# Attention's P V product: from two column groups and two rounds a step to four column groups and three rounds per two steps

## The chip, the cores and the metric

The kernel runs on one core of a Trainium2 chip. The metric is the device time of one execution in microseconds (us), the median over several runs; lower is better. Where the text names engines, PE is TensorE (PEld its weight loads, which the profile lists by themselves), DVE is VectorE, ACT is ScalarE, POOL is GpSimd and SP is the engine that issues the DMAs.

## The reference

One transformer-like block over 2048 tokens of width 512: adaptive layer norm and 32-head attention with 16 channels a head, then a second modulated layer norm and a token-shift MLP. The part that the change touches:

```python
qkv = (x @ wqkv).reshape(B, S, 3, H, Dh).transpose(2, 0, 3, 1, 4)   # S=2048, H=32, Dh=16
q, k, v = qkv[0], qkv[1], qkv[2]
scores = einsum("bhqd,bhkd->bhqk", q, k) * (Dh ** -0.5)
p = softmax(scores, axis=-1)
o = einsum("bhqk,bhkd->bhqd", p, v)                # "P V" below
return o.transpose(0, 2, 1, 3).reshape(B, S, D) @ wo
```

The products are computed to nearly fp32 precision: an fp32 operand is split into a coarse part and a remainder, and products of the parts are added up.

## The kernel before

**Tiling.** Queries come in 4 chunks of 512 (`ci`); heads come in 16 pairs. A unit is one chunk with one head pair, so there are 64 units. Within a unit the 2048 keys are walked in 16 tiles of 128; one key tile of one unit is a step, numbered `s` from 0 to 1023. A step does the following for its two heads `j`:

- L883: two score matmuls `sc` (keys by queries, 128 x 512), which stand in different row groups of PE.
- L867: beside them two matmuls `mb` for the step 24 further on. Their only purpose is the row maximum of each query, which DVE takes at L863 and which is later put into the score operands as an additional row.
- L879: ACT takes the exponential of each score tile and writes it as a 32-bit integer into the tile `pt`. `pt` has five buffers, so step `s` takes the buffer of step `s - 5`.
- L931 (`p_low`): POOL rewrites the low 16 bits of every element of `pt` in place as an fp16 number. The upper 16 bits already read as a (tiny) fp16 number. So `pt` holds P in two fp16 halves, interleaved. When the schedule expects POOL to be over 0.8 us later than ACT, ACT does the work instead, in two pieces of 512 columns (it shows under the helper's line L114).
- L946 (`pv_part`): the P V matmuls. `v` stands in `vst`, in 128 columns for the upper and 128 for the lower half. A head's 64 columns are three bf16 parts of v (16 columns each), a column of ones (which gives the softmax denominator) and zeros. For the lower half the same columns are stored again, multiplied by 2^-39. Each matmul has 64 weight columns, 512 moving columns and writes 64 partitions of one PSUM bank, head 0 the upper and head 1 the lower 64. A pair of matmuls for the two heads is called a round here. A step has two rounds: `(s, 0)` with the upper halves of P and `(s, 1)` with the lower halves, which needs `p_low` to be done. 1024 steps give 2048 rounds, 4096 matmuls.

After a unit, ACT copies the bank out (L960), PE transposes it (`ot`, L971), and DVE and POOL add the three parts up and divide by the sum (L978, L988, L982).

**What sets the order.** One Python scheduler (`Sched`) writes the instructions of all engines in a fixed order; it keeps a modelled time for each engine. The attention loop walks blocks of three score pairs (`GRP`, one and a half steps). A block is emitted as: its rows (`sc` and `mb`), then the P V rounds (`col`) that belong to the block two before (`LAG`), then "fill" work on PE, for which each step has a fixed budget. Fill is everything else: in the first chunk the q, k and v projections and the preparation of the later weights, in chunks 1 to 3 the output projection and the MLP of the chunk before, and the `ot` transposes. PE, ACT, DVE and POOL execute their lists in order, so a late instruction holds up all that stands behind it on its engine. When the modelled bank or P half is not ready in time, `gap` puts in fill work earlier. After the last step, the MLP of the last chunk runs by itself.

**Where v comes from.** `v_weights` (L707) loads and splits the columns of `wqkv` for v, in two groups of 256; `v_tiles` (L667) multiplies, ACT, DVE and POOL make the three bf16 parts (L700 to L704) and the result goes to DRAM (`Vs`). It comes back as `vst`, 1 MB for a unit. The first v tiles must be back before the first P V round.

Of the kernel before, what the change touches and what calls it, by code (L numbers as in the profile page):

```python
# [33 lines left out]
VLO = 2.0 ** -39  # L34
# [13 lines left out]
CROW, CCOL, CIN, CMID, COUT = 232.0, 249.0, 105.0, 95.0, 67.0  # L48
# [6 lines left out]
GRP = 3  # L55
LACT = 800.0
# [231 lines left out]
def kernel(ctx, tc, A_x, A_wqkv, A_wo, B_w1, B_w2, B_w3, B_w4, c, w_mod, out):  # L288
# [44 lines left out]


# [5 lines left out]
    dve.memset(mhalf, -0.5)  # L340
    mone = con.tile([P, 4], F32, name="mone")
# [10 lines left out]
    Vs = dr.tile([NP, P, NKT, 256], BF16, name="Vs")  # L352
# [174 lines left out]
    npool = [0]  # L527
# [122 lines left out]

    vt = []
    for i in range(NV):
        t = qp.tile([P, H // 4, 2, 2, 64], BF16, name=f"vt{i}")
        for l in range(2):
            pool.memset(t[:, :, l, :, 48:64], 0.0)
            pool.memset(t[:, :, l, :, 48:49], VLO if l else 1.0)
        vt.append(t)
# [9 lines left out]
    def v_tiles(w, a, kts):  # L667
        wh, wl = halves(w, KT)
        for kt in kts:
# [11 lines left out]
            v = w[:, :, 0]  # L681
# [3 lines left out]
            def rest(v=v, b3=b3, r=r, b=b):  # L685
                dve.tensor_tensor(r, b3, v[:, :, :, 0:16], op=OP.subtract)
                sch.free(b)

            def store(kt=kt, w=w):
                vrs[0] -= 1  # L690

                def gone():
                    vlive.remove(kt)
                    if kt % 4 == 3:
                        done.add(("v", a, kt // 4))
                e = sch.dma(dma.dma_start, Vs[8 * a:8 * a + 8, :, kt, :].rearrange("a p n -> p a n"),
                            w.rearrange("p a l b n -> p a (l b n)"))
                sch.after(e, gone)

            sch.chain(("A", cA(256), lambda v=v, b3=b3: act.activation(v[:, :, :, 0:16], b3, AF.Copy)),  # L700
                      ("D", cD(256), rest),
                      ("A", cA(256), lambda v=v, r=r: act.activation(v[:, :, :, 16:32], r, AF.Copy)),
                      ("G", cG(256), lambda v=v, r=r: pool.tensor_tensor(v[:, :, :, 32:48], r, v[:, :, :, 16:32], op=OP.subtract)),
                      ("A", cA(768), lambda v=v, w=w: act.activation(w[:, :, 1, :, 0:48], v[:, :, :, 0:48], AF.Copy, scale=VLO)),  # L704
                      (None, 0, store), prio=VP, bank=b)

    def v_weights(a):  # L707
        return split_weights([A_wqkv[:, 2 * D + a * 256:2 * D + (a + 1) * 256]])
# [23 lines left out]
    def pieces_load():  # L732
        yield lambda: ("v", 0, 2) in done
        for i, (nm, src, nk, n) in enumerate(pieces):
            if i == order["wo"][0]:
                yield from mod_gen((2, garow, 0.0))
# [4 lines left out]
            for c in range(2):  # L741
                yield sch.wait(5000.0)
# [4 lines left out]
    def pieces_gen():  # L747
        while True:
# [7 lines left out]
            ops = []  # L756
            if nm in rows:
                ops.append(("G", cG(), lambda f=f, r=rows[nm]: pool.tensor_tensor(f, f, r, op=OP.mult)))
# [39 lines left out]
    for g in (mod_cols(), ln1_T(), qk_first(hi, lo), weights_gen(), qkv_gen(0, 1), qkv_gen(1, len(todo))):  # L798
        sch.add(g)
# [35 lines left out]
    def load_v(u):  # L835
        vst[u] = at.tile([P, NKT, 2, 128], BF16, name="vst", tag="vst", bufs=2)
        if u > 1:
            sch.dma(dma.dma_start, vst[u].rearrange("p k l n -> p k (l n)"), Vs[units[u][1]])

    def load_first_v(u, i):  # L840
        k = slice(4 * i, 4 * i + 4)
        sch.dma(dma.dma_start, vst[u][:, k].rearrange("p k l n -> p k (l n)"), Vs[units[u][1], :, k])
# [95 lines left out]
    def pv_part(s, i):  # L938
        u, kt = divmod(s, NKT)
        if kt == 0 and i == 0:  # L940
            pv[u] = ap_.tile([P, CH], F32, name="pv", tag="v", bufs=1)
        p, v = pt[s].bitcast(F16), vst[u]

        def mms():
            for j in range(2):
                te.matmul(pv[u][64 * j:64 * j + 64, :], v[:, kt, i, 64 * j:64 * j + 64], p[:, j, 1 - i::2],  # L946
                          start=(kt == 0 and i == 0), stop=(kt == NKT - 1 and i == 1), skip_group_check=True)
        e = sch.put("P", CCOL, 0.0, mms)
        if i:
            pt.pop(s)  # L950
            e_low.pop(s)
            if kt == NKT - 1:
# [11 lines left out]
    def o_fin(u, ac, ready):  # L964
# [9 lines left out]
        sm = at.tile([P, 8, DH], F32, name="sm", tag="sm", bufs=2)  # L974
        rc = at.tile([P, 8, 1], F32, name="rc", tag="rc", bufs=2)

        def sums():
            dve.reduce_sum(sm, bv[:, :, 0:48].rearrange("p th (a d) -> p th d a", a=3), axis=AX.X)  # L978
            sch.free(b)

        def fin():
            pool.tensor_tensor(osb[ci][:, :, pr * 32:pr * 32 + 32].rearrange("p t (h d) -> p t h d", d=DH),  # L982
                              sm.rearrange("p (t h) d -> p t h d", h=2),
# [489 lines left out]
```

## Time and profile before

| what | value |
|---|---|
| runs | 2198.15 us median of 3 (2196.1 to 2198.7) |
| profiled execution | 2190.31 us, of which the span is 2188.5 us |
| PE busy | 2070.5 us, 95% of the span |
| POOL busy | 1735.1 us, 79% |
| DVE busy | 1638.3 us, 75% |
| ACT busy | 1533.1 us, 70% |
| first P V matmul | at 107.8 us |
| last P V matmul | starts at 2023.1 us |

The page gives busy times by engine and by groups of equal instructions (line, engine, operation, output<-input, count, then busy us and mean ns of one, then idle time of the engine just before them and its releasers). A matmul's duration in the trace is its latency, about 0.39 us for 512 columns; successive matmuls overlap, so their cost is read from the distance between starts. A view of stages gives busy time of each engine in a window. The chain of waits is followed back from the last instruction, at each step to what released it. Times within the trace count from the start of the span.

### The profile page before, as it was taken

What the parts mean: (1) busy time and instruction counts of PE and PEld (TensorE: products, weight loads), DVE (VectorE), ACT (ScalarE), POOL (GpSimd) and SP (SyncE); (2) the same over time, 40 slices, a digit from 0 to 9 for tenths busy, and PEclk for the clock granted to TensorE, in tenths of its full rate; (3) what the DMA queues carried; (4) which work ended last, traced back from release to release, by engine and by line L of the source; (5) the groups of instructions that cost most, each with busy time, mean ns of one, the idle gap of its engine ahead of it and who ended that gap; (6) DMA issues with size and microseconds to landing.
All of it is one profiled execution on the core that took longest, in us unless ns stands there. A gap on an engine that the chain in (4) does not pass through costs nothing.

```text
span 2188.5 us, 37190 instructions
## 1 busy us (share of the span) xinstructions
PE 2070.5 (95%) x12400; PEld 1162.6 (53%) x12400; DVE 1638.3 (75%) x2916; ACT 1533.1 (70%) x3268; POOL 1735.1 (79%) x1680
## 2 busy tenths in 40 slices
PE   6889999998899999999999999999899999999899
PEld 4645554554445555554445545555455555554688
DVE  6757777778898877778997877777888777773654
ACT  6456886668868777767767778677677767868353
POOL 3358897689978988888879989788779988888341
PEclk9889999999999999999999999999999999999999
DMA  5788887577453443535434344344524543443332
GB/s 199 190 240 263 238 220 210 170 206 218 129 181 95 114 145 103 153 94 167 99 91 114 95 125 133 105 114 104 162 77 114 151 115 92 137 95 116 135 136 82
DMA packets 201711, 313.36 MB, mean 143 GB/s; under 512 B 85520, under 2 KB 137232, under 8 KB 177296
## 3 DMA queue, kind: packets, MB, share of 16 engines
q1 hardware_dynamic: 201520, 310.98, 50.0%
q8 instruction: 99, 1.62, 0.3%
q14 instruction: 92, 0.75, 0.1%
HBM read 243.27 MB, written 67.11 MB: 142 GB/s over the span
## 4 chain that ended last, share of the span: by engine, by line
PE 67%; DVE 10%; POOL 7%; ACT 6%; DMA 6%; issue 3%; SPq 1%; POOLq 0%; ACTq 0%; DVEq 0%
PE pv L946 18%; PE mb L867 12%; PE sc L883 10%; PE w L320 7%; PE w L318 6%; PE w L316 6%; POOL pt L931 4%; DVE mx L863 4%; ACT pt L879 3%; DMA vst<-Vs 1%; SPq L93 1%; PE ot L971 1%; DMA wst<-in_A_wqkv_dram 1%; DMA wr<-Ws 1%; DMA kst<-Ks 1%
## 5 line engine op out<-in xcount | busy, mean ns | idle before, releaser
L863 DVE TENSOR_REDUCE mx<-mb 128x1 f32<-128x512 f32 x2048 | 1282.6, 682 | 295.9 <-PE mb L867 273.2
L931 POOL TENSOR_SCALAR pt<-pt 128x1024 f16<-128x1024 uint16 x1007 | 1339.6, 1363 | 198.8 <-ACT pt L879 194.8
L879 ACT ACTIVATE pt<-sc 128x512 int32<-128x512 f32 x2048 | 1078.1, 601 | 385.0 <-PE mb L867 322.3
L867 PE MATMUL mb<-kst,qtl 48*128 48x512 f32 x2048 | 722.0, 448 | 41.1 <-DMA kst<-Ks 9.2
L883 PE MATMUL sc<-qtl,kst 64*128 64x512 f32 x2048 | 693.9, 439 | 5.6 <-DVE sm L978 2.3
L946 PE MATMUL pv<-pt,vst 128*64 128x512 f16 x4096 | 610.7, 399 | 32.0 <-POOL pt L931 25.2
L867 PEld LDWEIGHTS mb<-kst,qtl 48*128 48x128 f32 x2048 | 341.3, 195 | 202.6 <-DVE mx L863 43.2
L883 PEld LDWEIGHTS sc<-qtl,kst 64*128 64x128 f32 x2048 | 334.4, 187 | 140.5 <-issue 45.0
L946 PEld LDWEIGHTS <-vst 128*64 128x64 bf16 x4096 | 178.9, 108 | 341.8 <-issue 265.3
L316 PE MATMUL w<-A,wr 128*128 128x256 f32 (+2 forms) x576 | 174.7, 303 | 3.0 <-ACT A L310 3.0
L318 PE MATMUL w<-A,wr 128*128 128x256 f32 (+2 forms) x576 | 175.9, 305 | 1.5 <-DVE A L306 1.3
L320 PE MATMUL w<-A,wr 128*128 128x256 f32 (+2 forms) x576 | 172.7, 300 | 0.0
L1223 POOL TENSOR_TENSOR g<-xs,g 128x256 fp32r<-128x256 f32 (+2 forms) x144 | 103.7, 721 | 81.1 <-ACT g L1222 80.7
L318 PEld LDWEIGHTS w<-A,wr 128*128 128x128 f32 x576 | 111.6, 194 | 37.0 <-issue 34.1
L316 PEld LDWEIGHTS w<-A,wr 128*128 128x128 f32 x576 | 111.8, 194 | 29.3 <-issue 18.3
L320 PEld LDWEIGHTS w<-A,wr 128*128 128x128 f32 x576 | 111.6, 194 | 23.7 <-issue 23.7
L316 PE MATMUL w<-wr,g 128*128 128x512 f32 x288 | 121.9, 423 | 0.1
L320 PE MATMUL w<-wr,g 128*128 128x512 f32 x288 | 120.6, 419 | 0.3 <-POOL g L1223 0.3
L318 PE MATMUL w<-wr,g 128*128 128x512 f32 x288 | 118.1, 410 | 0.0
L1232 DVE SCALAR_TENSOR_TENSOR sq<-sq,w 128x256 f32<-128x256 f32 (+1 forms) x108 | 43.4, 403 | 71.3 <-ACT xs L1228 63.4
L1238 POOL TENSOR_TENSOR xs<-xs,sq 128x256 f32<-128x256 f32 (+1 forms) x108 | 75.9, 704 | 5.7 <-ACT sq L1237 5.2
L1143 POOL TENSOR_TENSOR trs<-tmv,mhalf 128x1 f32<-128x1 f32 x48 | 33.5, 701 | 54.1 <-DVE tmv L1140 54.1
(130 smaller groups left out, 2049.1 us busy)
## 6 DMA issues: line engine op xcount, KB each, us to landing
wr<-Ws SPq DMA_DIRECT2D x80, 1024.0 KB, 5.2
vst<-Vs SPq DMA_DIRECT2D x62, 1024.0 KB, 6.5
kst<-Ks SPq DMA_DIRECT2D x126, 384.0 KB, 6.7
Vs<-vt SPq DMA_DIRECT2D x32, 512.0 KB, 4.4
qtl<-Qs SPq DMA_DIRECT2D x128, 96.0 KB, 4.8
Ws<-wq SPq DMA_DIRECT2D x40, 256.0 KB, 5.6
Ws<-wst SPq DMA_DIRECT2D x40, 256.0 KB, 5.1
wst<-in_B_w_dram SPq DMA_DIRECT2D x36, 256.0 KB, 5.4
```

The source lines that it names most:

```text
L316: te.matmul(o, lh, rh, start=first, stop=False)
L318: te.matmul(o, lh, rl, start=False, stop=False)
L320: te.matmul(o, ll, rh, start=False, stop=last)
L863: end = sch.crit("D", 605, e + PX, lambda: dve.reduce_max(mxs[u][:, j, g, c:c + 1], b, axis=AX.X))
L867: return ready, lambda: te.matmul(b, lhs, kst[u % 3][r, c * CH:(c + 1) * CH], start=True, stop=True), after
L879: ea = sch.crit("A", 480, e + PX, lambda: act.activation(pt[s][:, j], b, AF.Exp))
L883: return ready, lambda: te.matmul(b, kst[u % 3][r, kt * P:(kt + 1) * P], qst[u][r], start=True, stop=True), after
L931: e_low[s] = XP["G"] + sch.crit("G", 1345, ready, lambda: pool.tensor_scalar(o, i, 0.5, 1.0, op0=OP.mult, op1=OP.mult))
L946: te.matmul(pv[u][64 * j:64 * j + 64, :], v[:, kt, i, 64 * j:64 * j + 64], p[:, j, 1 - i::2], start=(kt == 0 and i == 0), stop=(kt == NKT ...
L1223: ("G", cG(n), lambda: pool.tensor_tensor(lo, xs, hi, op=OP.subtract)), (None, 0, end))
L1232: dve.scalar_tensor_tensor(sq, sq, 1.0 / GELU_A, b, op0=OP.add, op1=OP.mult)
L1238: ("G", cG(n), lambda: pool.tensor_tensor(xs, xs, sq, op=OP.mult)), *tail_ops, bank=b)
```

## The change

**The P V matmuls.** The upper halves keep their arithmetic: 64 columns of v for each head. They are now issued as two matmuls of 32 columns for each head, so a round with the upper halves of one step is four matmuls in four column groups of 32 (two of the four stream the same P). The lower halves use a single fp16 copy of v in place of the three bf16 parts: 16 columns of v and one column of ones. So one head and one step need only one column group, and a round with lower halves takes two heads of two steps, `s` and `s + 1`, at once: four matmuls with 17 or 25 weight columns (the 25 have 8 zero columns in front, so that results add up onto the right partitions). The order is upper `s`, upper `s + 1`, lower of both. The count goes from 2048 rounds of two matmuls to 1536 rounds of four, that is from 4096 to 6144 matmuls, each with a weight load.

**A bound for fp16.** For v to fit fp16, the columns of the v weights are divided by a bound. `bounds` and the new part of `v_weights` form it from the modulation and the absolute weights: four DVE passes, eight fp32 matmuls with 256 columns (`vb`), some small DVE work and four POOL multiplications. The rows of `wo` are multiplied by the same bound later (four ACT passes), so that the output stays the same.

**Smaller parts.** `Vs` and `vst` have 192 columns in place of 256. Per v tile ACT makes the fp16 copy (256 columns) and no longer the copy by 2^-39 (768 columns). The sum over the three parts now takes the denominators along (136 in place of 128 outputs), and the reciprocal follows it. The constant that the schedule takes for a round goes from 249 to 240 ns, and the preparation of the later weights waits 3.5 us between loads in place of 5.

```diff
-CROW, CCOL, CIN, CMID, COUT = 232.0, 249.0, 105.0, 95.0, 67.0
+CROW, CCOL, CIN, CMID, COUT = 232.0, 240.0, 105.0, 95.0, 67.0
...
-    Vs = dr.tile([NP, P, NKT, 256], BF16, name="Vs")
+    Vs = dr.tile([NP, P, NKT, 192], BF16, name="Vs")
...
-            sch.chain(("A", cA(256), lambda v=v, b3=b3: act.activation(v[:, :, :, 0:16], b3, AF.Copy)),
+            sch.chain(("A", cA(256), lambda v=v, b3=b3: act.activation(v[:, :, :, 0:DH], b3, AF.Copy)),
+                      ("A", cA(256), lambda vl=vl, b3=b3: act.activation(vl[:, :, :, 8:8 + DH], b3, AF.Copy, scale=1.0 / VHI)),
                       ("D", cD(256), rest),
...
-                      ("A", cA(768), lambda v=v, w=w: act.activation(w[:, :, 1, :, 0:48], v[:, :, :, 0:48], AF.Copy, scale=VLO)),
...
+            sch.chain(("D", 1200, lambda x=f.bitcast(F32), t=t: dve.scalar_tensor_tensor(
+                t, x, -1.0, x, op0=OP.mult, op1=OP.max)), mark(keys[i]), ready=e)
+        yield lambda: keys[0] in done and keys[1] in done and "gb" in done and sch.room()
+        b = dbank("vb")[:, :256]
+        for k in range(KT):
+            te.matmul(b, gb[:, k], ab[k // 2][:, k % 2 * 256:k % 2 * 256 + 256], start=(k == 0), stop=(k == KT - 1))
...
+                sch.chain(("G", cG(), lambda f3=f3: pool.tensor_tensor(f3, f3, vb[:, None, :].to_broadcast([P, 2, 256]),
+                                                                       op=OP.mult)),
+                          *split_chain(f, w[:, 0, c], w[:, 1, c], mark(keys[2 + i])), ready=sch.T["D"] + XX)
...
-                yield sch.wait(5000.0)
+                yield sch.wait(3500.0)
...
-    def pv_ready(s, i):
+    def pv_ready(s, lo):
 
-        return e_low[s] if i else max(e_hi.pop(s), v_free[0] if s % NKT == 0 else 0.0)
+        return max(e_low[s], e_low[s + 1]) if lo else max(e_hi.pop(s), v_free[0] if s % NKT == 0 else 0.0)
...
             for j in range(2):
-                te.matmul(pv[u][64 * j:64 * j + 64, :], v[:, kt, i, 64 * j:64 * j + 64], p[:, j, 1 - i::2],
-                          start=(kt == 0 and i == 0), stop=(kt == NKT - 1 and i == 1), skip_group_check=True)
+                for i in range(2):
+                    r = 64 * j + 32 * i
+                    if lo:
+                        n = 9 + DH if i else 1 + DH
+                        c = 128 + 32 * j + 9 + DH
+                        te.matmul(acc[r:r + n, :], v[:, kt + i, c - n:c].bitcast(F16), pt[s + i].bitcast(F16)[:, j, 0::2],
+                                  start=False, stop=kt == NKT - 2, skip_group_check=True)
+                    else:
+                        te.matmul(acc[r:r + 32, :], v[:, kt, r:r + 32], pt[s].bitcast(F16)[:, j, 1::2],
+                                  start=kt == 0, stop=False, skip_group_check=True)
...
-        if i:
-            pt.pop(s)
-            e_low.pop(s)
+        if lo:
+            for i in range(2):
+                pt.pop(s + i)
+                e_low.pop(s + i)
...
+    pvs = [x for s in range(0, NS, 2) for x in ((s, 0), (s + 1, 0), (s, 1))]
...
-        col = [divmod(x, 2) for x in blocks[k - LAG] if x >= 0] if k >= LAG else []
+        if k >= LAG and (k % CPER == 0 or not blk):
+            x = (blocks[min(k - LAG, len(blocks) - 1)] or [-1])[-1]
+            while pvs and 2 * (pvs[0][0] + pvs[0][1]) < x:
+                col.append(pvs.pop(0))
```

**How the order moves on PE, in the middle of the third chunk.** Here are the P V rounds of one block before: three rounds, each with a weight load and a matmul for each head (the number behind a name tells tiles apart, so pt_17189 is one step's P).

```order
L946 LDWEIGHTS vst_17023
L946 MATMUL pv_17270<-pt_17189,vst_17023 64x512 [waits Activation_49]
L946 LDWEIGHTS vst_17023
L946 MATMUL pv_17270<-pt_17189,vst_17023 64x512
L946 LDWEIGHTS vst_17023
L946 MATMUL pv_17270<-pt_17189,vst_17023 64x512 [waits Pool_49]
L946 LDWEIGHTS vst_17023
L946 MATMUL pv_17270<-pt_17189,vst_17023 64x512
L946 LDWEIGHTS vst_17023
L946 MATMUL pv_17270<-pt_17202,vst_17023 64x512
L946 LDWEIGHTS vst_17023
L946 MATMUL pv_17270<-pt_17202,vst_17023 64x512
```

And here a block of the change at the same unit: the upper halves of one step, then the first two matmuls of the round with the lower halves of two steps.

```order
L1024 LDWEIGHTS vst_18335
L1024 MATMUL pv_18602<-pt_18521,vst_18335 32x512
L1024 LDWEIGHTS vst_18335
L1024 MATMUL pv_18602<-pt_18521,vst_18335 32x512
L1024 LDWEIGHTS vst_18335
L1024 MATMUL pv_18602<-pt_18521,vst_18335 32x512
L1024 LDWEIGHTS vst_18335
L1024 MATMUL pv_18602<-pt_18521,vst_18335 32x512
L1021 LDWEIGHTS vst_18335
L1021 MATMUL pv_18602<-pt_18508,vst_18335 17x512 [waits Pool_49]
L1021 LDWEIGHTS vst_18335
L1021 MATMUL pv_18602<-pt_18521,vst_18335 25x512 [waits Pool_49]
```

A step's first two rounds (upper and lower) stood side by side before; now the lower half of the earlier step (pt_18508) stands behind the upper half of the later one (pt_18521), and its buffer is given back that much later. Blocks now have one, two or three rounds, where nearly all had three.

**On PE at the start.** Before, the first v tile follows the second chunk of k directly:

```order
L316 MATMUL k<-hT_110,wp 128x512
L318 MATMUL k<-hT_110,wp 128x512
L320 MATMUL k<-hT_110,wp 128x512
L316 MATMUL v<-wp,hT_109 128x256 [waits PE_49]
L318 MATMUL v<-wp,hT_109 128x256
```

With the change, the matmuls for the bound stand behind the first chunk of q, and the first v tile comes one chunk of k later than before.

```order
L321 MATMUL q<-hT_110,wp 128x512
L323 MATMUL q<-hT_110,wp 128x512
L747 MATMUL vb<-wab,gb 128x256 [waits DVE_49,PE_49]
L747 MATMUL vb<-wab,gb 128x256
L747 MATMUL vb<-wab,gb 128x256 [waits DVE_49]
L747 MATMUL vb<-wab,gb 128x256
L319 MATMUL k<-hT_111,wp 128x512 [waits PE_49,Activation_49]
```

All other work keeps its amount in every chunk: the fill of each chunk, the rows, and what runs after the last step. The share of `p_low` that the schedule gives to ACT grows from 17 steps to 36.

More of the change, by code (lines that the diff above doesn't have):

```diff
@@ L55 @@
 GRP = 3
+CPER = 1
 LACT = 800.0
@@ L340 @@
     dve.memset(mhalf, -0.5)
+    vcol = con.tile([P, 4], F32, name="vcol")
     mone = con.tile([P, 4], F32, name="mone")
@@ L525, in mod_cols, with bounds, g @@
             sch.chain(*[("D", 210, partial(diag, i)) for i in range(4)], mark(("mod", j)))
-    npool = [0]
+    gcol = qp.tile([P, 8], F32, name="gcol")
+    gb = qp.tile([P, KT, P], F32, name="gb")
+    def bounds():
+        yield lambda: ("mod", 0) in done and ("mod", 1) in done
+        def g():
+            dve.scalar_tensor_tensor(gcol, modcol, -1.0, modcol, op0=OP.mult, op1=OP.max)
+            dve.scalar_tensor_tensor(gcol[:, 0:4], gcol[:, 4:8], D ** 0.5, gcol[:, 0:4], op0=OP.mult, op1=OP.add)
+            dve.tensor_scalar(gb, gcol[:, 0:4, None].to_broadcast([P, KT, P]), 1.0 / (VMAX * VHI), None, op0=OP.mult)
+        sch.chain(("D", 800, g), mark("gb"))
     h32 = [sp.tile([P, CH], F32, name=f"h32{i}") for i in range(3)]
@@ L652 @@
     for i in range(NV):
[L653 to L656, printed above, removed]
+        t = qp.tile([P, H // 4, 192], BF16, name=f"vt{i}")
+        pool.memset(t, 0.0)
+        pool.memset(v_hi(t)[:, :, :, DH:DH + 1], VHI)
+        pool.memset(v_lo(t)[:, :, :, 8 + DH:9 + DH], 1.0)
         vt.append(t)
@@ new lines, in v_weights @@
+        st, ab, keys = [], [], [object() for _ in range(4)]
+        for i in range(2):
+            f, f3, e = yield from staged([kpn(src[i * 2 * P:(i + 1) * 2 * P])])
+            t = qp.tile([P, 512], F32, name="wab", tag="wab", bufs=2)
+            st.append((f, f3))
+            ab.append(t)
+            sch.chain(("D", 1200, lambda x=f.bitcast(F32), t=t: dve.scalar_tensor_tensor(
+                t, x, -1.0, x, op0=OP.mult, op1=OP.max)), mark(keys[i]), ready=e)
+        yield lambda: keys[0] in done and keys[1] in done and "gb" in done and sch.room()
@@ L710, in q_weights @@
+        yield lambda: keys[2] in done and keys[3] in done
+        return w
     def q_weights(a):
@@ L1419 @@
             sch.misc(e, max(sch.T["P"], sch.T[e]) + TOLE[e])
-        sch.fill(sum(budget(x // 2) / 2 for x in blk) if blk else 3 * TAILB[-1] / 2)
+        due += sum(budget(x // 2) / 2 for x in blk) if blk else 3 * TAILB[-1] / 2
+        if k % CPER == CPER - 1 or s0 < 0:
+            sch.fill(due)
+            due = 0.0
         if blk and blk[-1] == 2 * (NS // NC) - 1:
```

76 lines of the change are left out of this document (55 added, 21 removed).

## The prediction

> **What bounds the kernel now.** I read the page's totals first, then PE's timeline in one steady block, then busy times by stage, then the chain of waits.
>
> ```profile
> span 2188.5 us, 37190 instructions
> PE 2070.5 (95%) x12400; PEld 1162.6 (53%) x12400; DVE 1638.3 (75%) x2916; ACT 1533.1 (70%) x3268; POOL 1735.1 (79%) x1680
> ...
> L931 POOL TENSOR_SCALAR pt<-pt 128x1024 f16<-128x1024 uint16 x1007 | 1339.6, 1363 | 198.8 <-ACT pt L879 194.8
> ...
> L946 PE MATMUL pv<-pt,vst 128*64 128x512 f16 x4096 | 610.7, 399 | 32.0 <-POOL pt L931 25.2
> ```
>
> PE is the busiest engine, and P V is 610.7 us of its 2070.5 us; spread over 2048 rounds that is 0.298 us each, with tails that overlap other work. What a round costs in the stream shows PE's timeline (start us, us, engine and line, count):
>
> ```profile
> 1301.19 0.50 PE L867 MATMUL mb<-kst,qtl 48*128 48x512 f32 x1
> 1301.19 0.50 PE L883 MATMUL sc<-qtl,kst 64*128 64x512 f32 x1
> ...
> 1302.10 0.87 PE L946 MATMUL pv<-pt,vst 128*64 128x512 f16 x6
> 1302.90 0.50 PE L316 MATMUL w<-wr,g 128*128 128x512 f32 x1
> 1303.23 0.39 PE L318 MATMUL w<-wr,g 128*128 128x512 f32 x1
> 1303.46 0.40 PE L320 MATMUL w<-wr,g 128*128 128x512 f32 x1
> ```
>
> and the chain of waits around it:
>
> ```profile
> 1302.17 0.80 PE pv L946 x6
> ...
> 1309.50 0.57 PE pv L946 x4
> ...
> 1313.09 0.45 PE ot L971 x4
> ```
>
> Three rounds with the change of kind of work behind them take 0.80 us, two take 0.57: **one round is 0.23 us**. A single full-width matmul of 512 columns has the same distance (1303.23 to 1303.46). So two column groups beside each other already cost no more than one matmul.
>
> By chunk, from its first score matmul on (busy us of PE, PEld, DVE, ACT, POOL), and then three stretches almost without fill:
>
> ```profile
> 101.00:600.00 499.00, 460.56 (x2777) 248.09 (x2778) 364.09 (x631) 363.41 (x725) 411.75 (x354) 0.97 0.75 211
> 600.00:1063.00 463.00, 449.56 (x2804) 237.87 (x2804) 377.75 (x670) 344.50 (x763) 402.96 (x396) 0.99 0.47 130
> 1063.00:1539.00 476.00, 468.08 (x2851) 246.00 (x2848) 382.55 (x675) 350.82 (x760) 415.14 (x397) 1.00 0.42 110
> 1539.00:2019.00 480.00, 464.49 (x2811) 244.86 (x2809) 357.80 (x632) 352.19 (x764) 411.90 (x400) 0.99 0.42 119
> ...
> 578.00:599.70 21.70, 20.74 (x138) 9.78 (x136) 20.13 (x35) 17.41 (x35) 21.70 (x19) 1.00 0.41 100
> 1021.60:1042.50 20.90, 20.16 (x134) 9.37 (x132) 20.10 (x36) 17.39 (x36) 20.90 (x19) 1.00 0.47 98
> 1042.50:1063.50 21.00, 19.99 (x134) 9.40 (x132) 20.07 (x36) 17.37 (x36) 21.00 (x19) 1.00 0.45 100
> ```
>
> Over the 1918 us of attention PE is busy 1842.7 us (96%) and POOL 1641.8 us (86%). In units without fill, POOL is busy all the time and DVE 96%: there, a shorter PE gains nothing. The chain by line, for the same four windows:
>
> ```profile
> by line: PE pv L946 14.2%; POOL pt L931 12.1%; PE mb L867 9.5%; PE sc L883 7.4%; issue 5.4%; DMA vst<-Vs 5.3%; ACT pt L879 4.5%; SPq L93 3.6%; PE mr L580 3.2%; DMA wst<-in_A_wqkv_dram 3.0%; PE q L320 2.5%; POOL wst L769 2.5%; DMA wst<-in_B_
> ...
> by line: PE pv L946 21.6%; PE mb L867 14.3%; PE sc L883 11.3%; DVE mx L863 7.4%; PE w L320 7.2%; PE w L318 6.8%; PE w L316 6.8%; POOL pt L931 3.8%; ACT pt L879 2.7%; issue 2.7%; DMA wr<-Ws 1.9%; DMA kst<-Ks 1.9%; PE ot L971 1.1%; DVE xb L11
> ...
> by line: PE pv L946 25.2%; PE mb L867 16.7%; PE sc L883 13.1%; PE w L320 8.5%; PE w L316 8.5%; PE w L318 8.3%; DVE mx L863 4.0%; DMA wr<-Ws 1.9%; ACT pt L879 1.5%; PE ot L971 1.4%; POOL pt L931 1.2%; issue 1.0%; DVE sq L1232 1.0%; ACT sq L1
> ...
> by line: PE pv L946 22.5%; PE mb L867 13.5%; PE sc L883 12.4%; PE w L318 7.9%; PE w L320 7.9%; PE w L316 7.6%; DVE mx L863 4.3%; ACT pt L879 3.4%; issue 2.9%; POOL pt L931 2.1%; DMA wr<-Ws 1.9%; DMA kst<-Ks 1.9%; DVE sq L1232 1.4%; DVE xb L
> ```
>
> P V on the chain is 71, 100, 120 and 108 us (share times window), 399 us together, or 0.65 of its busy time. The first chunk is the one where POOL and DMA end many of the waits.
>
> **The change part by part.**
>
> *Fewer rounds.* 2048 rounds become 1536. If a round of four costs what a pair costs, 512 x 0.23 = 118 us leave PE. No row shows four matmuls beside each other, so the price of the new round is bounded. Below: 0.23, the distance of a single matmul and of a pair alike (four can't be quicker than one). Above: 0.46, two pairs one after the other. I take 0.23, because going from one to two column groups added nothing. The count of block boundaries stays, so the changes of kind of work on PE cost what they did.
>
> The 2048 additional matmuls and weight loads also have to be fed. A round now holds eight instructions. This row shows how closely the loads may stand:
>
> ```profile
> 1302.10 0.14 PEld L946 LDWEIGHTS <-vst 128*64 128x64 bf16 x4 [0.37 <-issue]
> ```
>
> Four loads of 64 columns, with the first pair of matmuls between them, run within 0.14 us; loads of 32 columns should not be slower. I cost the feeding at nothing beside a stream of 0.23 us; without that cover it is the slower rival below.
>
> *How much of the 118 us arrives.* By the chain 0.65 of it (77 us), by PE's busy share 0.96 of it (113 us). The chain leaves PE also in windows where PE is 98% busy, so the low figure is too strict; in the full POOL units and in the first chunk the high one is wrong. I take 0.81, **95 us**.
>
> POOL is the next to bind. The order gives 19 more steps of `p_low` to ACT: 19 x 1.33 = 25 us less on POOL (1339.6/1007 = 1.33), and 38 pieces of this row, 30 us, more on ACT:
>
> ```profile
> L114 ACT ACTIVATE pt<-pt x34: 753/791/889, 216.9 to 2021.3; 128x512 f16<-128x512 uint16 x34
> ```
>
> That makes POOL (1642 - 25)/(1918 - 95) = 89% and ACT (1411 + 30)/1823 = 79% busy. Both have room on average, and I cost the shift at nothing; what is lost in tight places is in the 0.81.
>
> *Later release of P.* The lower half of step s waits for step s + 1, so its buffer comes back later, while there are still five. By PE's order, in 319 of 1024 steps the exponential that takes the buffer of step s - 5 now waits for a round that stands behind the scores in the same block; in 191 of these it is the block's third exponential, which comes late enough anyhow, in 128 the second.
>
> ```profile
> 1301.76 1.58 ACT L879 ACTIVATE pt<-sc 128x512 int32<-128x512 f32 x3 [1.22 <-PE mb L867]
> ```
>
> Three in 1.58 us: the second would start at 1302.29, the third at 1302.82. The lower round would start at 1302.10 + 0.23 and end 0.39 later, about 1302.75. So 128 exponentials are delayed by some 0.45 us, 58 us of ACT's time. Behind each stand the block's third exponential, and behind that `p_low` on POOL and the score banks that PE's next rows need. ACT waited 1.22 us ahead of these three, which covers one such delay. Bounds 0 and 58; I take **6 us** of loss, nearer to the covered end.
>
> *The bound for fp16.* Eight fp32 matmuls of 256 columns: the nearest row has eight of 512 (16 records) in 9.0 us, so 4.5 us on PE. Four POOL multiplications at 1.31 (5.2 us) and four DVE passes at about 0.68 fall into stretches where these engines have idle time (first row: in the first 100 us POOL is busy 33.7 us, DVE 69.6).
>
> ```profile
> 0.00:100.00 100.00, 76.15 (x345) 54.05 (x346) 69.61 (x148) 50.34 (x86) 33.66 (x56) 0.90 0.60 190
> ...
> L517 PE MATMUL mr<-wm,silb 128*128 128x512 f32 x16 | 9.0, 724 | 9.4 <-DMA wm<-in_w_mod_dram 9.4
> ...
> L758 POOL TENSOR_TENSOR wst<-wst,gbrow 128x512 f32<-128x512 f32 x14 | 18.3, 1307 | 1.5 <-DMA Ws<-wq 1.5
> ...
> 100.93 6.79 DMA vst<-Vs
> ```
>
> The first P V round waits for v to come back from DRAM (the load at 100.93). v's weights now come later by the bound's chain (matmul, maximum, diagonal, reciprocal, multiplication, split), some 5 us, of which PE's order hides one chunk of k. Bounds 0 and 12 for all of it; I take **5 us**.
>
> *Edits costed at nothing.* `vst` and `Vs` carry a quarter less; DMA is on the chain with `vst<-Vs` 5.3% in the first chunk, mostly fixed waiting, so up to 5 us of gain. ACT's 32 copies of 768 columns become 256. The wider sum on DVE (136 for 128 outputs), the four `wo` passes and the earlier weight preparation move a few us of work that is hidden by the idle time of DVE (23% of attention) and ACT (26%); without that cover under 5 us. After the last step nothing changes.
>
> *Sum* on the profiled execution: 2190.3 - 95 + 6 + 5 = 2106 us. The runs' median lies 7.8 us above that execution, so the forecast is 2198.2 - 84 = **2114 us**.
>
> **The rivals.**
>
> *The gain arrives in full.* PE's 96% decides and the delays are absorbed: 113 us, plus up to 7 from DMA and the chunk end. 2198 - 113 = 2085. For it: the middle chunks' PE at 97 to 98%. Against it: the full POOL units, and 35% of the chain off P V's share. Chance 0.20.
>
> *POOL becomes the engine that ends the waits.* If POOL keeps today's share of idle time (its waits behind ACT and DVE don't shrink), attention takes 1617/0.856 = 1889 us, 29 less; 2198 - 29 = 2169. For it: POOL 100% in the units without fill. Against it: most of its idle time is waiting for exponentials that come sooner when PE is quicker. Chance 0.13.
>
> *The round of four costs more, and nothing is left.* If it costs 0.298, today's mean busy time of a round, PE saves 471 - 458 = 13 us, of which 0.81 cover the 11 us of losses: 2198. Against it: the second column group was free. Chance 0.07.
> The Trainium skill, TensorE: Matmul & The Clock Gate, section Measured speedup vs the span model, says three column tiles of 32 with 512 columns ran 2.38 times as fast as one after another, not 3 times. By an estimate from that page each further tile adds 0.13 of a matmul, a round of four takes 0.28 us, and the kernel about 2180 us; the trace of the pair shows no such addition.
>
> *Slower: PE can't be fed.* The closest row with eight instructions in one stretch is the group of four transposes (four loads, four matmuls) at 0.45 us on the chain above. If a round of four goes at that pace, or as two pairs (0.46), PE has 1536 x 0.45 = 691 in place of 471 us, 220 us more, which nothing hides: 2198 + 220 + 11 = 2429. It turns slower from a round of 0.30 us on. For it: no row shows eight in 0.23. Against it: the four loads in 0.14 us. Chance 0.08.
>
> **How the numbers follow.** Forecast 0.52 (own range 2090 to 2145), full gain 0.20, POOL 0.13, dearer round 0.07, slower 0.08. The range reaches from 2075 (full gain with the 7 us and a little) to 2185 (POOL, and a round slightly dearer). A difference of 0.2%, 4.4 us, is what a measurement here can tell. Faster: 0.52 + 0.20 + 0.13 and 0.04 of the dearer round, 0.89; the same 0.03; slower 0.08.
>
> **What would show it.** In the new profile, runs of three, two and one rounds should stand 0.80, 0.57 and 0.34 us long on the chain, with 6144 P V matmuls; a run of three near 1.5 would show the slower rival. POOL should be about 89% busy in attention with 988 `p_low`, PE still over 92%. First P V at 108 to 115 us, the stretch after the last step as long as before. Wrong would be: POOL over 95% with PE under 90%, ACT idle ahead of L947 for lower rounds by tens of us more than its 322 now, or a chunk that doesn't shrink.

## The result and the profile after

| | before | after |
|---|---|---|
| runs | 2197.12 us median of 4 (2194.01 to 2198.7) | 2139.14 us median of 4 (2135.28 to 2146.95) |
| profiled execution, span | 2190.31, 2188.5 us | 2135.28, 2133.2 us |

The change makes the kernel faster: the ratio is 0.9742 with an interval of 0.9713 to 0.9772. That is 58 us; 84 were forecast, with a range that holds the result.

First the page of the changed kernel: the totals, then the groups of `p_low` and of the two kinds of P V round (busy us, mean ns, idle time ahead).

```profile
span 2133.2 us, 41432 instructions
PE 2010.9 (94%) x14464; PEld 1126.3 (53%) x14464; DVE 1652.7 (77%) x2937; ACT 1548.1 (73%) x3310; POOL 1723.0 (81%) x1662
...
L947 ACT ACTIVATE pt<-sc 128x512 int32<-128x512 f32 x2048 | 1099.4, 602 | 345.1 <-PE mb L935 234.2
...
L999 POOL TENSOR_SCALAR pt<-pt 128x1024 f16<-128x1024 uint16 x988 | 1319.3, 1366 | 147.0 <-ACT pt L947 139.8
...
L1024 PE MATMUL pv<-pt,vst 128*32 128x512 f16 x4096 | 403.1, 402 | 1.2 <-DMA vst<-Vs 1.1
L1021 PE MATMUL pv<-pt,vst 128*17 128x512 f16 (+1 forms) x2048 | 222.1, 394 | 11.8 <-POOL pt L999 10.2
L1024 PEld LDWEIGHTS <-vst 128*32 128x32 bf16 x4096 | 95.8, 94 | 243.1 <-issue 219.7
```

L947 is the exponential (L879 before), L935 and L951 the scores, L1024 the upper rounds and L1021 the lower ones. P V's busy time rose from 610.7 to 625.2 us (403.1 + 222.1) although a quarter of its rounds is gone. A group's busy time is no price: each round now counts its full latency of 0.4 us. The price of a round stands in PE's timeline:

```profile
1299.49 0.50 PE L951 MATMUL sc<-qtl,kst 64*128 64x512 f32 x1
1299.93 0.41 PE L1024 MATMUL pv<-pt,vst 128*32 128x512 f16 x4
1300.16 0.40 PE L1021 MATMUL pv<-pt,vst 128*17 128x512 f16 x4
1300.39 0.40 PE L1024 MATMUL pv<-pt,vst 128*32 128x512 f16 x4
1300.72 0.38 PE L321 MATMUL w<-A,wr 128*128 128x256 f32 x1
...
1304.35 0.39 PE L951 MATMUL sc<-qtl,kst 64*128 64x512 f32 x1
1304.87 0.50 PE L935 MATMUL mb<-kst,qtl 48*128 48x512 f32 x1
```

Three rounds, four matmuls each, start 0.23 us apart, and the next work starts 0.79 us after the first of them. Over the whole trace the median distance from the first round of a run to the next work is 0.792 us for 319 runs of three, 0.565 for 191 of two and 0.339 for 191 of one: 0.226 us for each further round.

The stages, from the first score matmul, by chunk, then the stretch after the last score, and the attention as a whole (busy us of PE, PEld, DVE, ACT, POOL, then PE's granted clock, DMA share and GB/s):

```profile
103.60:586.50 482.90, 449.77 (x3272) 235.04 (x3271) 370.98 (x640) 362.88 (x738) 406.61 (x347) 0.98 0.71 200
586.50:1043.30 456.80, 439.86 (x3318) 233.55 (x3317) 377.16 (x670) 350.53 (x771) 397.97 (x393) 0.97 0.46 123
1043.30:1504.40 461.10, 446.07 (x3364) 234.80 (x3360) 382.64 (x675) 357.13 (x769) 411.00 (x393) 0.99 0.41 103
1504.40:1964.70 460.30, 444.46 (x3330) 235.37 (x3326) 356.48 (x633) 358.23 (x774) 407.22 (x396) 0.99 0.43 117
1964.70:2133.20 168.50, 149.62 (x823) 129.52 (x820) 86.15 (x162) 71.15 (x171) 58.94 (x81) 0.97 0.31 114
103.60:1964.70 1861.10, 1780.16 (x13271) 938.76 (x13270) 1487.25 (x2615) 1428.77 (x3049) 1622.80 (x1526) 0.98 0.50 137
```

| stretch, us | prologue | chunk 0 | chunk 1 | chunk 2 | chunk 3 | end |
|---|---|---|---|---|---|---|
| before (cut the same way) | 101.0 | 498.7 | 462.9 | 476.6 | 479.9 | 169.4 |
| after | 103.6 | 482.9 | 456.8 | 461.1 | 460.3 | 168.5 |
| difference | +2.6 | -15.8 | -6.1 | -15.5 | -19.6 | -0.9 |

If every removed round shortened its chunk, each chunk would lose 128 x 0.23 = 29.4 us. Chunk 1 loses a fifth of that, chunk 3 two thirds. PE's busy share in attention is 95.7% (1780.2 of 1861.1), almost what it was; yet in the timeline above the third pair of rows (1304.87) starts 0.52 us after the second. Matmuls that start up to 0.4 us apart show no idle time, so a share near 96% doesn't say that PE is full.

What ended the waits (us in total, times, longest):

```profile
ACT pt L947 <- PE mb L935: 234.2, 301, 3.1
...
POOL pt L999 <- ACT pt L947: 139.8, 218, 3.7
...
ACT pt L947 <- PE pv L1021: 84.3, 150, 1.8
...
PEld mb L935 <- DVE mx L931: 58.4, 148, 2.9
PEld mb L935 <- ACT pt L947: 56.5, 143, 5.4
```

The third row is new: the exponential waits for a lower round to release a buffer of P. On ACT's timeline it looks like this; the round of 1300.16 above ends at 1300.56, and the exponentials start at 1300.66:

```profile
1299.79 0.58 ACT L947 ACTIVATE pt<-sc 128x512 int32<-128x512 f32 x1
1300.66 1.09 ACT L947 ACTIVATE pt<-sc 128x512 int32<-128x512 f32 x2 [0.29 <-PE pv L1021]
```

The chain of chunk 2 by line now has little of P V, 17.9% for both lines where L946 had 25.2%, and ACT's exponentials 9.4% in place of 1.5%:

```profile
by line: PE mb L935 15.7%; PE pv L1024 12.7%; PE sc L951 11.0%; ACT pt L947 9.4%; DVE mx L931 7.0%; PE w L319 7.0%; PE w L321 6.9%; PE w L323 6.7%; PE pv L1021 5.2%; DVE sq L1311 2.1%; issue 1.9%; ACT sq L1306 1.4%; ACT xs L1307 1.3%; POOL 
```

So the question for the runs is where the other half of the 118 us went: late buffers, POOL, feeding the groups, or the amount of fill. Times below are medians; ratios are to the kernel before.

### The profile page after: what moved, and what is told of

The parts are those of the page before. It is cut to its first block, busy times and chain, and to the rows that moved or that the text cites. A ratio compares the mean times of both kernels' runs of the same rounds, so it can differ in the third digit from the quotient of the medians.

```text
span 2133.2 us, 41432 instructions
## 1 busy us (share of the span) xinstructions
PE 2010.9 (94%) x14464; PEld 1126.3 (53%) x14464; DVE 1652.7 (77%) x2937; ACT 1548.1 (73%) x3310; POOL 1723.0 (81%) x1662
## 4 chain that ended last, share of the span: by engine, by line
PE 59%; DVE 13%; ACT 12%; POOL 6%; DMA 5%; issue 3%; SPq 1%; POOLq 0%; DVEq 0%; ACTq 0%
PE mb L935 12%; PE pv L1024 9%; PE sc L951 8%; ACT pt L947 7%; PE w L321 6%; PE w L323 6%; PE w L319 6%; DVE mx L931 6%; PE pv L1021 4%; POOL pt L999 4%; SPq L96 1%; DMA wr<-Ws 1%; DMA wst<-in_A_wqkv_dram 1%; DVE sq L1311 1%; ACT pt L117 1%
## 5 line engine op out<-in xcount | busy, mean ns | idle before, releaser
L999 POOL TENSOR_SCALAR pt<-pt 128x1024 f16<-128x1024 uint16 x988 | 1319.3, 1366 | 147.0 <-ACT pt L947 139.8
L947 ACT ACTIVATE pt<-sc 128x512 int32<-128x512 f32 x2048 | 1099.4, 602 | 345.1 <-PE mb L935 234.2
L935 PE MATMUL mb<-kst,qtl 48*128 48x512 f32 x2048 | 761.9, 457 | 54.4 <-DVE sq L1311 10.5
L951 PE MATMUL sc<-qtl,kst 64*128 64x512 f32 x2048 | 728.2, 447 | 10.2 <-DVE qk L309 2.8
L935 PEld LDWEIGHTS mb<-kst,qtl 48*128 48x128 f32 x2048 | 347.7, 195 | 243.6 <-DVE mx L931 58.4
L951 PEld LDWEIGHTS sc<-qtl,kst 64*128 64x128 f32 x2048 | 337.0, 187 | 158.7 <-ACT pt L947 39.6
L1024 PE MATMUL pv<-pt,vst 128*32 128x512 f16 x4096 | 403.1, 402 | 1.2 <-DMA vst<-Vs 1.1
L1021 PE MATMUL pv<-pt,vst 128*17 128x512 f16 (+1 forms) x2048 | 222.1, 394 | 11.8 <-POOL pt L999 10.2
L1024 PEld LDWEIGHTS <-vst 128*32 128x32 bf16 x4096 | 95.8, 94 | 243.1 <-issue 219.7
L1317 POOL TENSOR_TENSOR xs<-xs,sq 128x256 f32<-128x256 f32 (+1 forms) x108 | 75.9, 703 | 15.8 <-ACT sq L1316 11.1
```

The source lines that it names most:

```text
L935: return ready, lambda: te.matmul(b, lhs, kst[u % 3][r, c * CH:(c + 1) * CH], start=True, stop=True), after
L947: ea = sch.crit("A", 480, e + PX, lambda: act.activation(pt[s][:, j], b, AF.Exp))
L951: return ready, lambda: te.matmul(b, kst[u % 3][r, kt * P:(kt + 1) * P], qst[u][r], start=True, stop=True), after
L999: e_low[s] = XP["G"] + sch.crit("G", 1345, ready, lambda: pool.tensor_scalar(o, i, 0.5, 1.0, op0=OP.mult, op1=OP.mult))
L1021: te.matmul(acc[r:r + n, :], v[:, kt + i, c - n:c].bitcast(F16), pt[s + i].bitcast(F16)[:, j, 0::2], start=False, stop=kt == NKT - 2, skip ...
L1024: te.matmul(acc[r:r + 32, :], v[:, kt, r:r + 32], pt[s].bitcast(F16)[:, j, 1::2], start=kt == 0, stop=False, skip_group_check=True)
```

## The experiments

### Does the feeding of four groups cost anything?

The kernel before, each matmul of 64 columns cut into two of 32: as many instructions in a round as after the change, with nothing else changed.

```diff
-                te.matmul(pv[u][64 * j:64 * j + 64, :], v[:, kt, i, 64 * j:64 * j + 64], p[:, j, 1 - i::2],
+                for r in (64 * j, 64 * j + 32):
+                    te.matmul(pv[u][r:r + 32, :], v[:, kt, i, r:r + 32], p[:, j, 1 - i::2],
```

> The kernel before with each P V matmul of 64 columns cut into two of 32, and nothing else: 2048 rounds of four in place of two, 4096 more matmuls and weight loads. If a round of four costs what a pair costs, as the changed kernel's trace says (0.226 us from round to round), it is the same as before within 0.4%, about 2197 us. If feeding eight instructions or four streams cost more, each 10 ns a round would show as about 20 us.

2204.17 us, ratio 1.002 (1.0002 to 1.0037). The kernel before took 2198.43 us in runs of the same chip; if all of the 5.7 us over it came from the rounds, that would be 3 ns for each of 2048. In the profiles chunks 2 and 3 are no longer than before (476.0 and 479.6 us, before 476.6 and 479.9), and the prologue, which has no P V round, is 5.9 us longer, so the rounds need not have cost anything. On the chain, runs of three rounds with 12 matmuls are as long as those with 6 were:

```profile
1299.74 0.79 PE pv L947 x12
...
1320.25 0.80 PE pv L947 x12
```

The feeding is free to within 3 ns a round. Both rivals that rest on a dearer round fall.

### Late buffers of P

A sixth buffer of P needs room in memory, so the number of staging tiles `NQ` goes from 7 to 5. The first kernel does only that, the second adds the buffer.

```diff
-NQ = 7
+NQ = 5
...
-            pt[s] = at.tile([P, 2, CH], I32, name="pt", tag="pt", bufs=5)
+            pt[s] = at.tile([P, 2, CH], I32, name="pt", tag="pt", bufs=6)
```

> The changed kernel with five in place of seven buffers for the q and k projections in the first chunk (NQ 5), which frees 4 KB a partition. It is the control for the next run, which needs that room, and differs from it in one number. All theories: the first chunk's order shifts a little; 2139 within 10 us, chunks 1 to 3 as in the changed kernel within 3 us.

> The control with six in place of five buffers for P; the order of all engines is the same as the control's, so only the waits for a free P buffer go. Late-buffer theory: ACT's wait for the lower rounds (84 us, 150 times in the changed kernel) falls below 10 us, and the kernel gets 15 to 30 us faster than the control. POOL theory (POOL is the engine that ends the waits, and the late buffers only fill its idle time): ACT's wait goes too, but under 6 us are won.

The control took 2148.92 us (0.9771, 0.9751 to 0.9791), 10 us over the change and just inside its span; its chunk 2 is 4 us longer than after the change, where at most 3 were expected. The kernel with six buffers took 2126.92 us (0.9687, 0.9649 to 0.9724): 22 us for the buffer. The exponential's group on the page with six buffers, and what its engine waited for in the view of that line:

```profile
L947 ACT ACTIVATE pt<-sc 128x512 int32<-128x512 f32 x2048 | 1078.9, 604 | 322.0 <-PE mb L935 299.8
```

```profile
  PE mb L935: 299.8, 343
  PE sc L951: 13.5, 20
  POOL osb L1061: 2.6, 1
  POOL pt L999: 2.2, 5
```

The wait for L1021 is gone, but most of its time has gone over to the wait for `mb` (228.2 us in the control). The total idle time ahead of the exponentials fell only from 344.6 us in the control to 322.0, by 23, and that is about what the kernel gained. **The row of one releaser is no price:** 83 us of it went, and 22 were won. The total of the group comes nearer here.

The same with other room: the vector of bounds and a scratch tile are laid into a weight tile that is done with, so that `NQ` need only go to 6.

```diff
-        vb = qp.tile([P, 256], F32, name="vb", tag="vb", bufs=1)
-        scr = qp.tile([P, P], F32, name="vscr", tag="vscr", bufs=1)
+        vb, scr = ab[0][:, 0:256], ab[0][:, 256:256 + P]
```

> The changed kernel with six P buffers as in e2_pt6, but with the room taken so that the first chunk suffers less: six in place of seven q and k buffers, and the bound's small tiles laid into a tile that is free by then. Late-buffer theory: the changed kernel's 2139 less the 22 us that e2_pt6 won over its control, so 2112 to 2124. If the 22 us came from the control's altered first chunk, it stays within 5 us of e2_pt6 or of the changed kernel.

2126.72 us, 0.968 (0.9655 to 0.9705): 12 us better than the change, some 3 us above the expected span. The idle time ahead of the exponentials is 331.8 us, 13 less than the change's 345.1. So the late buffers cost between 12 and 22 us, depending on what the room for the sixth costs; `NQ` 6 without the buffer wasn't run.

The counterpart, the kernel before with a buffer less:

```diff
-            pt[s] = at.tile([P, 2, CH], I32, name="pt", tag="pt", bufs=5)
+            pt[s] = at.tile([P, 2, CH], I32, name="pt", tag="pt", bufs=4)
```

> The kernel before with four in place of five P buffers, same order. Late-buffer theory: there too the exponentials now wait for P V rounds behind their scores (every step's buffer comes back one step later), so a new wait of ACT on L946 of 100 us or more appears and the time grows by 20 us or more, 1% over 2198. If PE's own saving alone made the changed kernel sensitive to late buffers, the kernel before loses under 8 us.

2204.55 us, 1.0035 (1.0019 to 1.0051): 6 us, where at least 20 were expected if a late buffer costs by itself. The second case came: the kernel before loses under 8, though the wait itself is longer than after the change (the page's group, then the view of waits):

```profile
L879 ACT ACTIVATE pt<-sc 128x512 int32<-128x512 f32 x2048 | 1113.2, 599 | 404.9 <-PE mb L867 261.0
```

```profile
ACT pt L879 <- PE pv L946: 96.8, 230, 6.0
```

Of those 96.8 us, 61 were there before as waits for `mb` (322.3, now 261.0), and the total rose from 385.0 to 404.9, by 20 us for 6 us of time, so the total of a group is no price either. A likely reason is that ACT has more time to spare in the old order (it is busy 74% of attention, 77% after the change); that isn't shown. The prediction's cover for this wait exists, but in the kernel before.

### POOL

The change with POOL's rewriting left out for head 1: `p_low` makes the lower half only for head 0, and head 1's lower rounds stream the upper half in its place. The number of matmuls stays.

```diff
-                o, i, 0.5, 1.0, op0=OP.mult, op1=OP.mult))
+                o[:, 0:CH], i[:, 0:CH], 0.5, 1.0, op0=OP.mult, op1=OP.mult))
...
-                        te.matmul(acc[r:r + n, :], v[:, kt + i, c - n:c].bitcast(F16), pt[s + i].bitcast(F16)[:, j, 0::2],
+                        te.matmul(acc[r:r + n, :], v[:, kt + i, c - n:c].bitcast(F16), pt[s + i].bitcast(F16)[:, j, j::2],
```

> The changed kernel with half of POOL's work on P: it makes the lower halves of the first head alone, and the second head's lower rounds stream the upper halves in their place (so the second head's result leaves the lower halves out). Same order on PE. POOL falls from about 88% to some 55% of attention. POOL theory: at least 25 us faster than the changed kernel. Late-buffer theory: under 10 us, and ACT's wait for the lower rounds stays near 84 us. Both binding: something between.

2123.38 us, 0.9641 (0.9616 to 0.9666): 16 us better than the change. POOL falls from 87% to 59% of attention (1082.4 of 1848.7):

```profile
103.60:1952.30 1848.70, 1776.25 (x13273) 943.92 (x13272) 1482.00 (x2615) 1425.05 (x3046) 1082.42 (x1526) 0.98 0.51 138
```

ACT's wait for L1021 stays at 84.6 us, so this is a second loss beside the buffers. In the profiles it lies in chunks 0 and 3 (6.8 and 5.7 us); chunks 1 and 2 stay within 2 us. Both removed together (`NQ` 5, six buffers, half of `p_low`):

> e2_pt6 (six P buffers, five q and k buffers) with half of POOL's work on P left out, as in e3_plow_half. If late buffers and POOL are two separate losses, it wins about the 16 us of e3_plow_half over e2_pt6's 2127, so 2105 to 2115. If the buffers' delay was what made POOL late, under 6 us: 2121 to 2127. With both gone, what is left against 2198 - 118 + 5 = 2085 belongs to other engines.

2115.83 us, 0.9624 (0.9601 to 0.9646), 11 us below six buffers alone, and 1 us above the expected span. Chunk 3 now is 450.3 us, 29.6 less than before, which is the full 29.4:

```profile
1488.20:1938.50 450.30, 437.40 (x3332) 233.78 (x3328) 355.47 (x633) 351.35 (x771) 271.16 (x395) 1.00 0.43 120
```

Chunks 0, 1 and 2 are 476.3, 450.1 and 456.6, that is 7, 16.6 and 9.4 us short of theirs, and the prologue is 4.2 us longer than before (105.2). So some 31 us (2115.8 less the 2085 of the full gain) are not explained by the buffers and this half of `p_low`. Three things in the record bear on them. The room (`NQ` 5) alone had cost the control 10 us. The mean granted clock of the four runs is 0.9675, that of the kernel before in the same runs 0.975; executions of one kernel get some 1.5 us longer for each 0.001 of clock (an estimate over all runs; those of the next kernel took 2117.7 us at 0.977 and 2131.1 at 0.967), so some 11 of the 31 us go with the clock, as cause or as a result of PE's waits. And in the last unit of chunk 1, which has almost no fill, DVE is now busy 19.87 of 20.40 us and POOL only 12.69; before, the unit took 21.1 us. There DVE is what is left to limit the unit, not POOL:

```profile
1011.20:1031.60 20.40, 19.45 (x170) 8.62 (x166) 19.87 (x37) 17.35 (x36) 12.69 (x18) 1.00 0.43 89
```

Does it help to hand `p_low` to ACT sooner? Six buffers and `NQ` 6 again, with the delay of POOL from which ACT takes over lowered:

```diff
-LACT = 800.0
+LACT = 300.0
```

> e5_m6 with the bound for giving a lower half to ACT cut from 0.8 to 0.3 us of modelled lateness, which moves a few more of them from POOL to ACT. POOL theory, which e3_plow_half gave 16 us of: POOL's load falls by only a few us, so 0 to 8 us faster than e5_m6. If ACT is as near to its end as POOL: slower by up to 10 us.

2128.29 us, 0.9675 (0.9647 to 0.9702), no difference to the 2126.72 with 800. 18 more steps go to ACT; POOL is busy 21 us less and ACT 20 us more, so it may be that ACT pays what POOL gains.

### The two constants and the traffic of v

The first two units take 72.4 us (88.3 before). Both constants put back, to see whether they did that:

```diff
-CROW, CCOL, CIN, CMID, COUT = 232.0, 240.0, 105.0, 95.0, 67.0
+CROW, CCOL, CIN, CMID, COUT = 232.0, 249.0, 105.0, 95.0, 67.0
...
-                yield sch.wait(3500.0)
+                yield sch.wait(5000.0)
```

> The changed kernel with the two numbers of the schedule set back: 249 ns a round and 5 us between the loads of later weights. If the first chunk's 16 us came with those numbers, it loses 8 to 16 us there; if they came with the smaller v transfers (DMA vst<-Vs was 30% of the chain in the first two units before, 5% after), the first two units stay at 72 us within 4 and the whole within 6 us of 2139.

2148.52 us, 0.9778 (0.9761 to 0.9794), 9 us over the change, where at most 6 were expected. The first two units stay at 71.5 us, so the constants aren't what shortened them. They move work over the border of the chunks: chunk 0 is 13 us shorter than after the change and chunk 1 21 us longer, so the gains by chunk in the table hold for the new constants alone. The first unit of chunk 1 takes 49.4 us here, with PE busy for 28.7 of them, because the preparation of the later weights is drained there.

```profile
578.10:627.50 49.40, 28.67 (x196) 14.47 (x192) 23.78 (x41) 25.17 (x49) 39.17 (x33) 0.76 0.71 221
```

Now the change with part of `v` loaded twice, which brings the bytes back to about what they were, by 70 additional DMAs:

```diff
+            dma.dma_start(vst[u][:, 0:5], Vs[units[u][1], :, 0:5])
...
+        dma.dma_start(vst[u][:, 4 * i:4 * i + 1], Vs[units[u][1], :, 4 * i:4 * i + 1])
```

> The changed kernel that loads part of v twice: one more key tile with each of the first eight loads of four, five more with each of the later loads of sixteen, so that it reads about as many bytes of v as the kernel before (by 70 more DMAs). If the smaller v transfers gave the first unit its 8 us (48.6 to 40.4), the first unit gets 4 to 8 us longer again and the whole 4 to 12 us slower; later units stay. If the reordered start gave it, under 2 us.

2180.53 us, 0.9914 (0.9889 to 0.9939): 41 us slower than the change, where 4 to 12 were expected. The first unit, before, after the change, and here:

```profile
101.00:149.60 48.60, 38.80 (x209) 22.32 (x208) 25.07 (x43) 30.05 (x60) 27.09 (x25) 0.83 0.87 245
```

```profile
103.60:144.00 40.40, 32.89 (x217) 19.19 (x216) 24.18 (x42) 26.16 (x57) 27.38 (x25) 0.87 0.89 249
```

```profile
108.10:155.70 47.60, 35.47 (x215) 20.04 (x214) 24.27 (x42) 26.24 (x57) 29.81 (x27) 0.78 0.77 218
```

The first unit is about as long as before again. Chunk 0 is 28 us longer than after the change, chunks 1 and 3 by 8 each, chunk 2 by 1. But the edit does a third thing beside adding bytes and DMAs. Both loads of a pair write the same part of `vst`, and the second is issued only after the first has landed; the DMA queue waits, with all loads that stand behind it. Its waits for `vst`, here and then after the change:

```profile
SPq L96 <- DMA vst<-Vs: 289.4, 79, 9.6
```

```profile
SPq L96 <- DMA vst<-Vs: 7.5, 5, 2.5
```

So the run doesn't price the bytes, nor the number of DMAs: the 41 us may be the price of this held-up queue. It shows that the first unit gets longer when v comes later, not that the smaller `vst` made it shorter. What the smaller `vst` is worth isn't measured.

### The amount of fill

Chunk 1 gained least. A step's budget of fill there was set when PE had more P V to do; a smaller one might fit better. With six buffers and `NQ` 6 as above:

```diff
-TAILB = (0.0, 500.0, 500.0, 540.0)
+TAILB = (0.0, 450.0, 490.0, 520.0)
```

> e5_m6 with less fill a step in chunks 1 to 3 (450, 490 and 520 in place of 500, 500 and 540 ns), which lays the same fill over more units: in chunk 1 three units without fill in place of four, in chunk 3 more in the last unit. POOL is busy all the time in units without fill and they can't shrink, so if that is a loss, 3 to 10 us faster than e5_m6's 2127, in chunks 1 and 3. If the fill then ends later than the next chunk needs it, slower by up to 10 us at the chunk's border.

2114.65 us, 0.9624 (0.9595 to 0.9653): another 12 us. Chunk 1 went from 456.4 us, with six buffers alone, to 442.7:

```profile
586.10:1028.80 442.70, 428.17 (x3318) 227.60 (x3317) 377.29 (x670) 347.95 (x775) 395.40 (x391) 0.99 0.47 127
```

The count of matmuls is the one of the change's own chunk 1, so no work is left over for later. 12.0 of these 13.7 us lie in two units, the fifth and sixth of the chunk (with six buffers alone, then with the smaller budget):

```profile
708.70:780.00 71.30, 66.38 (x469) 38.61 (x468) 49.69 (x93) 50.73 (x118) 58.38 (x64) 0.86 0.36 96
```

```profile
705.70:765.00 59.30, 57.30 (x448) 32.11 (x447) 48.74 (x91) 47.93 (x110) 55.89 (x62) 1.00 0.46 120
```

21 fewer matmuls of fill are a small part of that. In every run with the change's budgets PE waits there for weights from DRAM (2.2 to 3.9 us), and the granted clock drops around that wait. In the change itself:

```profile
740.24 0.44 PE L319 MATMUL w<-A,wr 128*128 128x128 f32 x1 [3.28 <-DMA wr<-Ws]
```

```profile
735.00:750.00 15.00, 11.72 (x66) 7.30 (x69) 6.21 (x13) 8.06 (x20) 8.73 (x12) 0.59 0.62 189
```

The kernel before has no such wait, and neither have the runs with the smaller budgets. The two units took 61.8 us before and 69.5 after the change, where fewer rounds should have made them 3.7 us shorter: 11 of the 23 us that chunk 1 lacks are lost here. The units without fill, which the expectation named, didn't bring the gain: the last four units of the chunk got fill and grew from 89 to 100 us, and ten others shrank by about as much.

The run's 2114.65 us are 24 us below the change and 84 below the kernel before (2198.37 in the same runs), faster than both. The same for chunk 0, on top:

```diff
-SC0 = (32, 900.0, 700.0)
+SC0 = (32, 900.0, 620.0)
```

> e11_m6_tail with the first chunk's fill thinned as well (620 in place of 700 ns a step after the 32nd), three units without fill in place of four there. 0 to 6 us faster than e11_m6_tail if such units are the loss, up to 10 slower if the first chunk's preparation ends late.

2115.36 us, 0.9617 (0.9595 to 0.9639): no difference. In the profile chunk 0 is 4 us shorter and chunk 1 7 us longer, 6 of them in its first unit.

## Why the prediction was right, and where it was off

**The price of a round** was right: 0.226 us where 0.23 was taken, and the run that cuts the pair into four shows it directly. The gross gain of 118 us holds. The rivals "dearer round" and "PE can't be fed" fall. The estimate from the page of the Trainium skill, TensorE: Matmul & The Clock Gate, section Measured speedup vs the span model, was 0.28 us a round and 2180 us for the kernel; neither is borne out.

**The share that arrives** was the mis-sized step: 0.81, or 95 us. Attention became 57 us shorter (1918 to 1861.1). Without some 6 us in the first two units that the rounds don't explain (below), the rounds brought about 51, or 0.43 of the 118, and that with the 9 us that hang on the new constants. It is below even the 0.65 of the chain, which the prediction called too strict. The result lies in the range because the range was wide, not because the losses were priced rightly. Both figures were read as a share that stays; but each us that leaves PE also moves the next limit nearer, and three losses then took part:

- *Late buffers*, costed at 6 us. The mechanism was named rightly (58 us of ACT's time in 128 cases were forecast, 84.3 us in 150 measured), the price wasn't: it is 12 to 22 us. The cover, ACT's idle time, was read from the kernel before, where it does cover such a wait (96.8 us of it cost 6 there); the change itself seems to use it up. The prediction's sign of being wrong, more idle time of ACT than the 322 us, did not show this loss: 234.2 us for `mb` and 84.3 for the lower rounds make 318.5.
- *POOL*, costed at nothing because of 11% of room on average. Its share came out as forecast (87%, forecast 89; 988 `p_low` as the order had it), but half of `p_low` removed brings 16 us, or 11 on top of the buffers. The rival "POOL ends the waits" would have given 2169; POOL is a limit in part of the units, not the limit: in the units without fill of chunk 1, where the prediction saw POOL busy all the time, a unit still takes 20.4 us with half of `p_low` gone, and DVE is busy nearly all of it.
- *Fill per unit*, hidden in the 0.81: 12 us of it could be had back by spreading the fill anew, most of them at one place in chunk 1 where PE now waits for weights and the clock is low. No term of the prediction stood for such a wait.

Added up these make 35 to 45 us (12 or 22 for the buffers, 11 for POOL on top of them, 12 for the fill), out of some 67 that did not arrive; all three were never removed in one run. For the rest no run names a cause. The granted clock and DVE are suspects: DVE fills the unit shown above, and its row maximum holds up the weight loads of `mb` for 58.4 us in the waits after the change. A run with less work on DVE wasn't tried, and it stays open. The rival "full gain" (2085) falls for the whole kernel, but chunk 3 shows it once the buffers and half of `p_low` are out of the way.

**The bound for fp16**: 5 us taken. The prologue to the first score matmul is 2.6 us longer and the first P V round starts at 110.1 us in place of 107.8, inside the span given. But profiles with the same prologue scatter by more (101.0, 106.9 and 108.6 us in the order before; 103.1 to 108.3 after the change), so the size of this term isn't shown.

**v's traffic** was costed at nothing, with up to 5 us of gain. The first two units are 15.9 us shorter. In the groups of PE in that stretch, q and k projections fell from 80 matmuls of 512 columns to 54 and v's from 65 of 256 to 51; at 0.23 and 0.12 us that is about 8 us of fill put into later units, less some 2 us for eight matmuls of the bound that stand there now. Another 3.7 are 16 fewer rounds. Some 6 us are left, of which v's part can't be told apart: the waits of P V for `vst` fell from 4.3 to 1.1 us, and the granted clock rose from 0.87 to 0.91.

**After the last step** 0.9 us changed, as said. **From the profiled execution to the median** the prediction carried 7.8 us over; after the change it is 3.9. The working itself was 29 us off (2106 forecast for the profiled execution, 2135.3 measured); that the median is only 25 off is luck.

## What to carry to other kernels

When work leaves the busiest engine, price what comes next before taking a share of the gain: give the ring of buffers one more place, take half the work from the engine behind it, and spread the filler anew, each in a run of its own. A cover read from the old kernel (idle time of an engine, room in a schedule) may be spent partly by the change itself. Look at the total idle time of the waiting group beside a new wait, since a wait named after one releaser can have been there under another name; the price still takes a run. And look in the trace of each such run whether the edit did only what it was meant to do: the second load of `v` held up a queue.

## What the runs showed of the hardware that was not expected

Four column groups of 17 to 32 columns with 512 moving columns cost what one full-width matmul costs: 0.226 us for four matmuls and four weight loads, with loads of about 94 ns each that overlap one another (4096 of them are busy for 95.8 us in all). A change of the kind of work costs about 0.1 us: from a single round's start to the next kind of work it is 0.34 us, against 0.226 to another round. In this program a DMA that writes where an earlier one is still writing is held back until that one has landed, and the queue with it: 79 waits, 289.4 us, in the run that loads part of v twice. And a wait of 3 to 4 us on PE stood beside a low clock: 0.59 granted from 735 to 750 us after the change (a wait of 3.28 us), 0.50 from 734 to 754 us with six buffers and `NQ` 6 (3.90 us), 1.00 from 735 to 750 us with the smaller budgets, where there is no such wait.
